# Strassen's seven products for two of the six row tiles in the output matmul of a gated convolution

## The chip, the cores and the metric

The kernel runs on one core of a Trainium2 chip, in float32 throughout. The metric is device time in microseconds, the median of several executions; here 1151.66 us before the change (three runs, 1151.52 to 1152.45). The span of a profile runs from the first to the last instruction, and is a little shorter than the execution's own time.

## What is computed

Two blocks in a row on a batch of 8 sequences of 3136 rows and 256 features: the real part of a two-dimensional Fourier transform, and a feed-forward block with a gate from a three-tap convolution.

```python
X = np.fft.fft(np.fft.fft(x, axis=1), axis=2).real
h = np.maximum(X @ w_in, 0.0)                   # (8, 3136, 1024)
conv_out += conv_w[k] * hp[:, k:k + S, :]       # k = 0, 1, 2; hp is h padded by one row
gate = 1.0 / (1.0 + np.exp(-conv_out))
return h * gate @ w_out                         # (8, 3136, 256)
```

## The kernel before, in words

The transform over the sequence is done by matmuls with cosine and sine tables on a folded input (sums and differences of mirrored rows, so that the tables are an eighth of their size). The transform over the features is folded into w_in: G holds w_in times the feature transform, so that X @ w_in becomes two products, one with the cosine half (tile pt) and one with the sine half (tile qt) of the sequence transform.

The second block is the long part. Each of the 8 batches is cut into 4 **chunks** of rows, each chunk into 8 **steps**, one per 128 of the 1024 hidden features: 256 steps (b, c, f). A step works on 768 or so rows (832 in the last chunk of a batch) in these parts:

- `seed` (ScalarE) writes the first feature's share into a PSUM bank pa, `products` (TensorE) adds the two products in pa and pb, `copies` (ScalarE) moves pb to SBUF as nb, and `combine` (VectorE, two instructions) forms the relu of pa + nb and of pa - nb: the row tile h, both ends of the sequence at once.
- `first_tap` (ScalarE), `middle` (a DMA with addition that GpSimd issues) and `last_tap` (VectorE) make the convolution in tile g; `sigmoid` (ScalarE) and `gate` (VectorE, g times h) finish it.
- `mm2` (TensorE) multiplies the gated step with w_out: g is the stationary operand, 128 rows at a time, and wout of 256 columns the moving one. A chunk has six such **row tiles**; their sums over the 8 steps stay in three PSUM banks po, two tiles in each. After the last step ScalarE copies the banks out and SyncE writes them to DRAM. The last chunk of each second batch has a seventh tile of leftover rows.

A matmul of float32 stands in the profile as two weight loads (PEld) and two passes (PE), so six row tiles are 12 passes of 256 columns.

The program is written as 261 **cycles** (the loop at the end of the function); each engine runs its own instructions strictly in the order written. Cycle t holds, in this order: sigmoid of step t-4, products and copies of step t+1, combine of step t, seed of t+2, first_tap of t, then what is hung on the place "dve" (the folds of the next batch, VectorE instructions of 0.6 to 1.2 us), last_tap of t-3, gate of t-4, what is hung on "late" (the sums that finish a piece of the next batch's sequence transform), middle of t, loads, and mm2 of step t-5, then transform matmuls (tile pd) of the next batch. So the mm2 of cycle t needs the gate that VectorE made in cycle t-1, and VectorE's combine of cycle t needs the products that TensorE made in cycle t-1, ahead of that cycle's mm2. VectorE can thus be about a cycle ahead of what TensorE needs next, and not more. The two PSUM banks pa, the one bank pb and the seven buffers of g set the same limits.

Of the kernel before, what the change touches and what calls it, by code (L numbers as in the profile page):

```python
# [9 lines left out]
F32 = mybir.dt.float32  # L10
# [3 lines left out]
ALU = mybir.AluOpType  # L14
# [23 lines left out]
def kernel(  # L38
# [10 lines left out]
    nc = tc.nc  # L49
    B, S, D = x.shape  # L50
    F = moe_w_in.shape[1]
    P = 128
# [21 lines left out]
    ebp = ctx.enter_context(tc.tile_pool(name="ebp", bufs=4))  # L74
# [6 lines left out]
    edp = ctx.enter_context(tc.tile_pool(name="edp", bufs=1, space=DRAM))  # L81
    psa = ctx.enter_context(tc.tile_pool(name="psa", bufs=2, space=PSUM))
    psb = ctx.enter_context(tc.tile_pool(name="psb", bufs=1, space=PSUM))
    psd = ctx.enter_context(tc.tile_pool(name="psd", bufs=1, space=PSUM))
    pso = ctx.enter_context(tc.tile_pool(name="pso", bufs=4, space=PSUM))

# [5 lines left out]
    def mm(o, l, r, start, stop):  # L92
        nc.tensor.matmul(o, l, r, start=start, stop=stop, skip_group_check=True)  # L93
# [149 lines left out]
    rp = ctx.enter_context(tc.tile_pool(name="rp", bufs=2))  # L243
    PQ, eb, er = {}, {}, {}
    ed = edp.tile([B, (RC // 2 + 1) * RC], F32, name="ed")

# [649 lines left out]
    def keep(s):  # L896
# [3 lines left out]
        if r.start < r.stop:  # L900
            nc.scalar.copy(out=left[:, f, b % 2 * LEFT:(b % 2 + 1) * LEFT], in_=gs[s][:, r])

    def mm2(s):
        b, c, f = s
        ch = chunks[c]
        tiles = [(gs[s][:, o:o + m], [(0, b, r, m)]) for o, r, m in ch.tiles]
        if ch.last and b % 2:
            tiles.append((left[:, f], [(i * LEFT, b - 1 + i, ch.rest[1], LEFT) for i in range(2)]))
        for i, (w, to) in enumerate(tiles):
            if f == 0 and i % 2 == 0:  # L910
                po[b, c, i // 2] = pso.tile([P, 2, D], F32, name="po", tag="po")
            pt = po[b, c, i // 2]
            mm(pt[:, i % 2, :], w, wout[:, f, :], f == 0 and i % 2 == 0, f == NF - 1)
            if f == NF - 1 and (i % 2 or i == len(tiles) - 1):
                del po[b, c, i // 2]
                osb = osp.tile([P, 2, D], F32, name="os", tag="os")
                for j in range(i - i % 2, i + 1):
                    nc.scalar.copy(out=osb[:, j % 2], in_=pt[:, j % 2])  # L918
                if i % 2:
                    r0, r1 = (tiles[j][1][0][2] for j in (i - 1, i))  # L920
                    nc.sync.dma_start(out=bass.AP(
                        tensor=out.tensor, offset=out.offset + (b * S + r0) * D,
                        ap=[[D, P], [(r1 - r0) * D, 2], [1, D]]), in_=osb)
# [3 lines left out]
        gs.pop(s)  # L927


    def keep_on(n):  # L930
# [77 lines left out]
    def at(cycle, where, fn):  # L1008
        side.setdefault((cycle, where), []).append(fn)
# [1 line left out]
    for i in (2, 3):  # L1011
        at((0, 0, 1, 3)[i], "pe", lambda i=i: blocks(i))
    at(0, "pool", store)
    at(0, "load", lambda: spread(0, range(1, len(chunks))))

    early, *rest = three(w_in[2].parts(0, 2, room))
    at(0, "first", early)
# [14 lines left out]
    def free(cycle):  # L1032
# [3 lines left out]
        taken.add(cycle)  # L1036
        return cycle

    feat = Feature()
    at(5, "load", feat.place)  # L1040
    at(8, "dve", feat.signs)
# [10 lines left out]
    for b in range(1, B):  # L1052
        begin, us, *_ = units(b)
        us = us[0:2] + us[5:7] + us[2:4] + us[7:] if b == 1 else us[0:4] + us[5:]

        c0 = ends[b] - 3 * (b == 1)
        n = per * b - (2 if b == 1 else 3) - c0
        at(max(c0, per * (b - 1) + 1), "pe", begin)
        cs = [c0 + i * n // len(us) for i in range(len(us) + 1)]
        if b > 1:  # L1060
            cs[1:] = [c + (-1 if i == len(us) else 1) * (c % NF == LAG % NF) for i, c in enumerate(cs[1:], 1)]
        for i, u in enumerate(us):
            k = cs[i + 1] - cs[i]
# [6 lines left out]
        at(cs[-1] - 2, "load", lambda b=b: spread(b, range(len(chunks) - 1)))  # L1070
        at(per * b + 1, "load", lambda b=b: spread(b, [len(chunks) - 1]))
    for b in range(1, B):
        ops, singles, pres = fold_ops(b)
        c0, n = ends[b - 1], ends[b] - ends[b - 1]
# [130 lines left out]
```

## Time and profile before

| | before |
|---|---|
| median of 3 runs | 1151.66 us |
| profiled execution | 1151.81 us, of it the span 1150.0 us |
| granted TensorE clock | 1.000 |
| busy in the span: PE, PEld | 1133.3 us, 888.3 us |
| busy in the span: VectorE (DVE), ScalarE (ACT), GpSimd (POOL) | 967.9, 894.8, 389.6 us |

The page names each group of instructions by line, engine, operation and tiles (out<-in), with busy time, the mean length of one, and the idle time ahead of it. Lengths overlap: a VectorE instruction may start before the one ahead has ended, and a matmul's end is modelled. What an engine spends on one instruction is therefore read from start to start. The timeline gives these starts. The view by windows gives each engine's busy time between two moments.

### The profile page before, as it was taken

The numbers are of one execution on the slowest core, as the hardware profiler recorded it, in microseconds if no ns is written. First come the engines' busy times: TensorE is split into PE (matmuls) and PEld (weight loads), VectorE is DVE, ScalarE is ACT, GpSimd is POOL, SyncE is SP. The second block draws the span as 40 slices with busy tenths as digits, with TensorE's granted clock in tenths as the row PEclk, the third lists the DMA queues.
The fourth block names the chain that finished last, engine by engine and source line by source line (L and its number), as shares of the span: only waits on it lengthen the run. The fifth ranks groups of instructions, "written<-read, shape, count | busy, mean of one in ns | idle before, by whom it ended". The sixth has DMA issues, their size and how long they took to land.

```text
span 1150.0 us, 15064 instructions
## 1 busy us (share of the span) xinstructions
PE 1133.3 (99%) x4824; PEld 888.3 (77%) x4824; DVE 967.9 (84%) x1452; ACT 894.8 (78%) x1707; POOL 389.6 (34%) x486
## 2 busy tenths in 40 slices
PE   6999999999999999999999999999999999999998
PEld 4777877787778777777778777777778777777777
DVE  8999899988888989898878879888886777777775
ACT  3788778877787778787878777887887777888884
POOL 6425523552434252524143332422222112222223
PEclk9999999999999999999999999999999999999999
DMA  9787975876767677756676766866664656666664
GB/s 249 184 130 158 170 179 110 186 166 143 172 133 151 128 188 157 163 123 150 139 174 134 159 139 129 179 124 123 138 131 87 129 123 142 132 137 124 127 117 100
DMA packets 107676, 167.49 MB, mean 146 GB/s; under 512 B 32175, under 2 KB 62921, under 8 KB 107598
## 3 DMA queue, kind: packets, MB, share of 16 engines
q0 software_dynamic: 42240, 115.87, 52.3%
q1 hardware_dynamic: 64616, 50.53, 15.8%
q8 instruction: 38, 0.62, 0.2%
q10 hardware_dynamic: 741, 0.14, 0.1%
q14 instruction: 41, 0.33, 0.1%
HBM read 37.80 MB, written 25.74 MB: 55 GB/s over the span
## 4 chain that ended last, share of the span: by engine, by line
PE 94%; DVE 3%; ACT 1%; issue 1%; DMA 0%; POOL 0%; DVEq 0%; ACTq 0%
PE po L93 58%; PE pb L93 15%; PE pa L93 15%; PE pd L93 6%; DVE g L863 1%; DVE h L848 1%; DVE g L890 1%; DMA raw<-in_moe_w_in_dram 0%; DVE wout L661 0%; ACT nb L840 0%; DVE raw L667 0%; ACT os L918 0%; ACT g L882 0%; ACT pa L819 0%; ACT g L854 0%
## 5 line engine op out<-in xcount | busy, mean ns | idle before, releaser
L93 PE MATMUL po<-wout,g 128*128 128x256 f32 x3072 | 705.0, 379 | 1.2 <-DVE g L890 1.1
L93 PEld LDWEIGHTS po<-wout,g 128*128 128x128 f32 x3072 | 581.5, 190 | 142.2 <-issue 18.5
L858 POOL DMA_DIRECT2D g<-h x256 | 220.1, 860 | 713.5 <-ACT g L854 474.8
L840 ACT ACTIVATE nb<-pb 128x386 f32<-128x386 f32 (+3 forms) x512 | 228.0, 500 | 196.8 <-PE pb L93 195.8
L848 DVE CUSTOM_DVE_ANT_0 h<-pa,nb 128x386 f32<-128x386 f32 (+3 forms) x512 | 265.4, 560 | 49.3 <-PE pa L93 30.3
L890 DVE TENSOR_TENSOR g<-g,h 128x770 f32<-128x770 f32 (+1 forms) x248 | 240.8, 971 | 64.1 <-ACT g L882 62.3
L863 DVE SCALAR_TENSOR_TENSOR g<-h,cw,g 128x770 f32<-128x770 f32 (+1 forms) x256 | 265.4, 1037 | 1.9 <-DMA g<-h 1.9
L882 ACT ACTIVATE g<-g,cw 128x770 f32<-128x770 f32 (+3 forms) x264 | 246.3, 936 | 18.0 <-DVE g L863 17.9
L854 ACT ACTIVATE g<-h,cw 128x770 f32<-128x770 f32 (+1 forms) x256 | 244.3, 954 | 0.0
L93 PE MATMUL pb<-qt,G 127*128 127x387 f32 (+2 forms) x512 | 213.6, 498 | 1.5 <-ACT nb L840 1.1
L93 PE MATMUL pa<-pt,G 128*128 128x387 f32 (+2 forms) x512 | 212.1, 495 | 0.9 <-ACT pa L819 0.7
L819 ACT ACTIVATE pa<-eb,ge 128x387 f32<-128x387 f32 (+2 forms) x256 | 155.4, 607 | 0.6 <-ACT ft L585 0.3
L93 PEld LDWEIGHTS pa<-pt,G 128*128 128x128 f32 x512 | 96.6, 189 | 75.7 <-issue 19.0
L129 POOL DMA_INDIRECT xh<-in_x_dram,idx x64 | 102.9, 1608 | 19.3 <-issue 10.4
L93 PEld LDWEIGHTS pb<-qt,G 127*128 127x128 f32 x512 | 91.7, 190 | 9.1 <-ACT nb L840 2.8
L93 PE MATMUL pd<-tab,w 98*128 98x197 f32 (+2 forms) x448 | 95.3, 317 | 0.0
L93 PEld LDWEIGHTS pd<-tab,w 98*128 98x128 f32 (+1 forms) x448 | 80.5, 191 | 8.2
L918 ACT COPY os<-po 128x256 f32<-128x256 f32 x196 | 57.5, 394 | 6.3 <-PE po L93 6.3
L176 POOL COPY w<-xh 98x4 f32<-98x4 f32 (+1 forms) x30 | 45.0, 1501 | 6.8 <-DVE xh L170 6.7
L154 DVE TENSOR_TENSOR xh<-xh 98x1020 f32<-98x1020 f32 (+1 forms) x32 | 38.7, 1211 | 0.5 <-DMA xh<-in_x_dram,idx 0.4
L165 DVE TENSOR_TENSOR xh<-xh 98x1024 f32<-98x1024 f32 (+1 forms) x32 | 38.9, 1216 | 0.1
L398 DVE TENSOR_TENSOR as<-as,pd 128x196 f32<-128x196 f32 x14 | 5.0, 358 | 20.4 <-ACT as L394 20.3
(150 smaller groups left out, 427.7 us busy)
## 6 DMA issues: line engine op xcount, KB each, us to landing
g<-h POOLq DMA_DIRECT2D x192, 385.0 KB, 4.0
g<-h POOLq DMA_DIRECT2D x64, 416.0 KB, 4.1
out_dram<-os SPq DMA_DIRECT2D x96, 256.0 KB
xh<-in_x_dram SPq DMA_DIRECT2D x16, 784.0 KB
eb<-ed SPq DMA_DIRECT2D x16, 193.5 KB
raw<-in_moe_w_in_dram SPq DMA_DIRECT2D x4, 512.0 KB
raw<-in_moe_w_out_dram SPq DMA_DIRECT2D x1, 2048.0 KB
eb<-ed SPq DMA_DIRECT2D x8, 209.0 KB
```

The costliest lines, as they stand in the source:

```text
L93: nc.tensor.matmul(o, l, r, start=start, stop=stop, skip_group_check=True)
L129: nc.gpsimd.indirect_dma_start(out=xh[b, h][0:NP, 7 - m].rearrange("p q d -> p (q d)"), out_offset=None, in_=bass.AP(tensor=x.tensor, offs ...
L176: nc.gpsimd.tensor_copy(w[k, 0:2, qs, 0], t()[k, s:s + 2, :, 0])
L819: act(pa[s][:, 0:n], eb[b, c], AF.Copy, scale=ge[:, f:f + 1])
L840: act(nb[s][:, i, cols], p[:, cols], AF.Copy, scale=-1.0 if i else 1.0)
L848: nc.vector._custom_dve(TENSOR_ADD_SAT, out=to, in0=a[:, cols], in1=c[:, i, cols], s0=BIG, s1=0.0)
L854: act(gs[s], hs[s][:, 0:n], AF.Copy, scale=cw[:, 0, s[2]:s[2] + 1])
L858: nc.gpsimd.dma_start(out=gs[s], in_=hs[s][:, 1:1 + n], accum_op=ALU.add)
L863: stt(out=g, in0=h[:, k:k + n], scalar=cw[:, k, f:f + 1], in1=g, op0=ALU.mult, op1=ALU.add)
L882: act(gs[s][:, c], gs[s][:, c], AF.Sigmoid, scale=cw[:, 1, s[2]:s[2] + 1])
L890: vt(g, g, h[:, 0:r.stop], op=ALU.mult)
L918: nc.scalar.copy(out=osb[:, j % 2], in_=pt[:, j % 2])
```

## The change

In 23 of the 32 chunks (all from batch 1's second chunk on, but for the last chunk of batches 1, 3, 5 and 7) the row tiles 4 and 5 are no longer multiplied with w_out step by step. Two steps f-1 and f, f odd, are taken together: the 256 rows of the two tiles by 256 features form a 2 by 2 array of blocks of 128 by 128, a11 to a22, and the two steps' rows of w_out with their two column halves form b11 to b22. Strassen's scheme in Winograd's form gives the product with seven block products in place of eight:

- `forms` (VectorE, once): four combinations of w_out's blocks, in tile tw.
- `sums` (VectorE, in each odd step's cycle, ahead of last_tap): four combinations of the a blocks, 128x128 each, in tile sv, which has one buffer.
- `mm7` (TensorE): three products of 128 columns right after the four other row tiles of the odd step, and four more, which need the sums, at the head of the next step's mm2 (list `due`). All seven are added up over the four pairs of steps in two PSUM banks x and y.
- at the chunk's end ScalarE copies one block, and `end` (VectorE, in the next cycle, behind gate and "late") makes the four output blocks with four instructions that read PSUM; SyncE then writes them.

The banks po per such chunk are four (two for the row tiles 0 to 3, x and y) of the pool's four. Some buffers are given up for room (tile eb from 4 to 3, rt from 2 to 1), and the eb loads are issued a few cycles later.

```diff
+    def sums(s):
+        (a11, a12), (a21, a22) = blocks_of(s)
+        t = sums_of[s] = svp.tile([P, 4, P], F32, name="sv", tag="sv")
+        vt(t[:, 0], a21, a22, op=ALU.add)
+        vt(t[:, 1], a21, a11, op=ALU.subtract)
+        vt(t[:, 2], t[:, 1], a22, op=ALU.add)
+        vt(t[:, 3], a12, t[:, 2], op=ALU.subtract)
...
+    def mm7(s):
...
+        mm(x[:, 0], a11, wout[:, f - 1, 0:P], m == 0, last)
+        mm(x[:, 1], a12, wout[:, f, 0:P], False, last)
+        mm(y[:, 0], a22, TW[4][:, m], m == 0, last)
+        def rest():
+            t = sums_of.pop(s)
+            mm(y[:, 1], t[:, 0], TW[5][:, m], False, last)
+            mm(y[:, 2], t[:, 1], TW[7][:, m], False, last)
+            mm(x[:, 2], t[:, 2], TW[6][:, m], False, last)
+            mm(x[:, 3], t[:, 3], wout[:, f, P:D], False, last)
+        due.append(rest)
...
+        nc.scalar.copy(out=o[:, 1, 0], in_=x[:, 0])
+        def end():
+            twice = lambda w: w.unsqueeze(1).to_broadcast([P, 2, P])
+            vt(o[:, 0], twice(o[:, 1, 0]), x[:, 1:3], op=ALU.add)
+            vt(o[:, 1], twice(o[:, 0, 1]), y[:, 1:3], op=ALU.add)
+            vt(o[:, 0, 1], o[:, 1, 0], x[:, 3], op=ALU.add)
+            vt(o[:, 1], twice(o[:, 1, 1]), y[:, 0:2], op=ALU.add)
+            write(b, c, (4, 5), osb)
+        ends_of.append(end)
     def mm2(s):
...
+        for fn in due:
+            fn()
...
+        if seven(s):
+            tiles = tiles[:4]
...
         run("dve")
+        if t >= LAG and seven(steps[t - LAG]) and steps[t - LAG][2] % 2:
+            sums(steps[t - LAG])
         if 0 <= t - 3 < n:
             last_tap(steps[t - 3])
```

On TensorE, a cycle pair in the first chunk of batch 2 as it stood before (an odd step's mm2, then an even one's; pd is the next batch's transform, x6 means six in a row):

```order
L93 MATMUL po<-wout,g 128x256 [waits DVE_49]
L93 MATMUL po<-wout,g 128x256 x5
L93 MATMUL pd<-tab_109,w 128x197 [waits DVE_49,PE_49,Activation_49]
L93 MATMUL pb<-qt,G 128x387 [waits PE_49]
L93 MATMUL pa<-pt,G 128x387 [waits Activation_49]
L93 MATMUL po<-wout,g 128x256 x6
```

The same place after the change:

```order
L94 MATMUL po<-wout,g 128x256 [waits DVE_49]
L94 MATMUL po<-wout,g 128x256 x3
L94 MATMUL po<-wout,g 128x128 [waits DVE_49,PE_49]
L94 MATMUL po<-wout,g 128x128
L94 MATMUL po<-tw,g 128x128
L94 MATMUL pd<-tab_112,w 128x197 [waits DVE_49,PE_49,Activation_49]
L94 MATMUL pb<-qt,G 128x387 [waits PE_49]
L94 MATMUL pa<-pt,G 128x387 [waits Activation_49]
L94 MATMUL po<-tw,sv 128x128 x3
L94 MATMUL po<-wout,sv 128x128
L94 MATMUL po<-wout,g 128x256 x4
```

Twelve matmuls of 256 columns became eight of 256 and seven of 128; four of the seven stand behind the next step's products.

On VectorE, the same chunk's cycle with a fold (xh) before:

```order
L848 ISA h<-pa,nb 128x386 [waits DVE_49,PE_49,Activation_49]
L848 ISA h<-pa,nb 128x386 [waits Activation_49]
L169 TENSOR_TENSOR xh<-xh 98x512
L170 TENSOR_TENSOR xh<-xh 98x512
L863 TENSOR_SCALAR g<-h,cw,g 128x770 [waits DMASW4_49]
L890 TENSOR_TENSOR g<-g,h 128x770 [waits Activation_49]
```

And after, where DVE_49 is VectorE's own semaphore:

```order
L849 ISA h<-pa,nb 128x386 [waits DVE_49,PE_49,Activation_49]
L849 ISA h<-pa,nb 128x386 [waits Activation_49]
L170 TENSOR_TENSOR xh<-xh 98x512
L171 TENSOR_TENSOR xh<-xh 98x512
L933 TENSOR_TENSOR sv<-g 128x128 [waits DVE_49,PE_49]
L934 TENSOR_TENSOR sv<-g 128x128
L935 TENSOR_TENSOR sv<-sv,g 128x128 [waits DVE_49]
L936 TENSOR_TENSOR sv<-g,sv 128x128 [waits DVE_49]
L864 TENSOR_SCALAR g<-h,cw,g 128x770 [waits DMASW4_49]
L891 TENSOR_TENSOR g<-g,h 128x770 [waits Activation_49]
```

The four sums stand ahead of last_tap and gate, and two of them wait for VectorE's own instruction just ahead. Where a chunk has ended, the next cycle holds behind its gate:

```order
L891 TENSOR_TENSOR g<-g,h 128x770 [waits Activation_49]
L971 TENSOR_TENSOR os<-os,po 128x256 [waits DMAHW3_49,DMAHW4_49,DMAHW0_49,PE_49]
L972 TENSOR_TENSOR os<-os,po 128x256 [waits DVE_49]
L973 TENSOR_TENSOR os<-os,po 128x128 [waits DVE_49]
L974 TENSOR_TENSOR os<-os,po 128x256 [waits DVE_49]
L849 ISA h<-pa,nb 128x386 [waits Activation_49] x2
```

Nothing stood between gate and combine there before.

More of the change, by code (lines that the diff above doesn't have):

```diff
@@ L242 @@
     turn = const.tile([P, 3, 2], F32, name="turn")
[L243 removed]
+    rp = ctx.enter_context(tc.tile_pool(name="rp", bufs=1))
     PQ, eb, er = {}, {}, {}
@@ L901, in keep, with seven, forms @@
             nc.scalar.copy(out=left[:, f, b % 2 * LEFT:(b % 2 + 1) * LEFT], in_=gs[s][:, r])
+    TW = {}
+    due, ends_of = [], []
+    def seven(s):
+        b, c, f = s
+        return (b, c) > (1, 0) and not (chunks[c].last and b % 2)
+    def forms(i):
+        one, two = wout[:, 0:NF:2], wout[:, 1:NF:2]
+        b11, b12, b21, b22 = one[:, :, 0:P], one[:, :, P:D], two[:, :, 0:P], two[:, :, P:D]
+        if i == 0:
+            t = erp.tile([P, 4, NF // 2, P], F32, name="tw", tag="er")
+            TW.update({k: t[:, j] for j, k in enumerate((5, 7, 6, 4))})
+        k, x, y = ((5, b12, b11), (7, b12, b22), (6, b11, TW[7]), (4, b21, TW[6]))[i]
+        vt(TW[k], x, y, op=ALU.subtract)
@@ new lines, in blocks_of @@
+    def blocks_of(s):
+        b, c, f = s
+        o = [chunks[c].tiles[i][0] for i in (4, 5)]
+        return [[gs[b, c, k][:, v:v + P] for k in (f - 1, f)] for v in o]
+    sums_of = {}
+    def sums(s):
[5 more added lines that the diff above has]
+        vt(t[:, 3], a12, t[:, 2], op=ALU.subtract)
@@ L905, in mm2 @@
         ch = chunks[c]
+        done = ends_of[:]
+        for fn in due:
+            fn()
+        due.clear()
+        ends_of.clear()
         tiles = [(gs[s][:, o:o + m], [(0, b, r, m)]) for o, r, m in ch.tiles]
@@ L919, in mm2 @@
                 if i % 2:
[L920 to L923, printed above, removed]
+                    write(b, c, (i - 1, i), osb)
                 else:
@@ L926, in mm2 @@
                         (nc.scalar if j and s == steps[-1] else nc.sync).dma_start(out=rows[b_ * S + r:b_ * S + r + m, :], in_=osb[p0:p0 + m, 0])
-        gs.pop(s)
+        if not seven(s):
+            gs.pop(s)
+        elif f % 2:
+            mm7(s)
+            gs.pop(s)
+            gs.pop((b, c, f - 1))
+        for fn in done:
+            fn()
     def keep_on(n):
@@ L1013 @@
     at(0, "pool", store)
-    at(0, "load", lambda: spread(0, range(1, len(chunks))))
+    at(0, "load", lambda: spread(0, range(1, len(chunks) - 1)))
+    at(NF, "load", lambda: spread(0, [len(chunks) - 1]))
     early, *rest = three(w_in[2].parts(0, 2, room))
@@ L1037, in free @@
         return cycle
+    for i in range(4):
+        at(per + 6 + i, "dve", lambda i=i: forms(i))
     feat = Feature()
```

23 lines of the change are left out of this document (20 added, 3 removed).

## The prediction

> **What bounds the kernel now.** I read the page first: busy times, then the chain that ended last.
>
> ```profile
> span 1150.0 us, 15064 instructions
> PE 1133.3 (99%) x4824; PEld 888.3 (77%) x4824; DVE 967.9 (84%) x1452; ACT 894.8 (78%) x1707; POOL 389.6 (34%) x486
> PE 94%; DVE 3%; ACT 1%; issue 1%; DMA 0%; POOL 0%; DVEq 0%; ACTq 0%
> ```
>
> TensorE carries 94% of the chain, so matmul time saved is time saved, as long as nothing else becomes late. VectorE, which gets the new work, is second with 84%. A share over the whole span hides the stages, so next come windows: seven chunks each (batch 2 to the third chunk of 3; batch 4 to the third of 5; batch 6 to the third of 7), the two chunks of batch 1 that change, the chunk ahead of these, and a stretch of batch 0. Columns: window, length, busy time of PE, PEld, DVE, ACT, POOL.
>
> ```profile
> 340.60:580.40 239.80, 239.80 (x1026) 190.01 (x1025) 210.98 (x317) 189.70 (x352) 87.07 (x97) 1.00 0.70 153
> 617.20:855.00 237.80, 237.80 (x1013) 187.92 (x1012) 203.87 (x307) 189.67 (x351) 66.43 (x87) 1.00 0.66 138
> 891.80:1119.40 227.60, 227.60 (x948) 177.76 (x947) 170.67 (x242) 185.18 (x337) 49.64 (x66) 1.00 0.62 127
> 232.60:268.50 35.90, 35.90 (x158) 28.80 (x157) 31.85 (x50) 27.20 (x52) 17.54 (x16) 1.00 0.69 155
> 268.50:305.70 37.20, 37.20 (x164) 29.82 (x163) 31.29 (x49) 27.28 (x51) 8.79 (x11) 1.00 0.68 147
> 201.20:232.60 31.40, 31.38 (x129) 24.20 (x128) 30.34 (x45) 26.58 (x50) 17.80 (x20) 1.00 0.81 179
> 60.00:90.00 30.00, 28.90 (x115) 21.08 (x114) 29.83 (x47) 25.36 (x54) 9.19 (x17) 1.00 0.83 134
> ```
>
> TensorE never rests in the first five, at full clock (1.00). VectorE's room differs: 28.8 us in the first stretch of seven chunks (4.1 per chunk), 33.9 in the second, 56.9 in the third. The last row shows the other regime: VectorE busy for 29.83 of 30 us, and there TensorE waits.
>
> Who waits for whom in each regime is in the timeline:
>
> ```profile
> 67.63 0.95 DVE L890 TENSOR_TENSOR g<-g,h 128x770 f32<-128x770 f32 x1
> 68.64 2.86 PE L93 MATMUL po<-wout,g 128*128 128x256 f32 x12
> 604.02 1.01 DVE L890 TENSOR_TENSOR g<-g,h 128x832 f32<-128x832 f32 x1
> 604.01 2.75 PE L93 MATMUL po<-wout,g 128*128 128x256 f32 x12
> 606.60 0.59 PE L93 MATMUL po<-wout,left 128*128 128x256 f32 x2
> 608.68 2.75 PE L93 MATMUL po<-wout,g 128*128 128x256 f32 x12
> ```
>
> In batch 0 the gate ends at 68.58 and mm2 starts 0.06 later: TensorE follows VectorE. In batch 3 the gate ends at 605.03 and its mm2 starts at 608.68: VectorE **leads by 3.6 us**. This lead is what it may lose before TensorE feels it.
>
> **TensorE's gain.** 12 passes start within 606.60 - 604.01 = 2.59 us, 0.216 per pass of 256 columns. Per pair of steps, 8 such passes (1.727 us) go and 14 passes of 128 columns come. By columns alone that would be 0.108 each, but each needs its own weight load of 128 columns. What a load costs when the pass is short shows where the passes have 98, 99 and 1 columns, and 196 or 197; of the first two groups I quote the first and the last row of five and of six at even distance:
>
> ```profile
> 30.99 0.30 PEld L93 LDWEIGHTS po<-tab,w 99*128 99x128 f32 x2
> 31.43 0.30 PEld L93 LDWEIGHTS po<-tab,w 98*128 98x128 f32 x2
> 21.34 0.30 PEld L93 LDWEIGHTS po<-dm,win 128*128 128x128 f32 x2
> 21.90 0.19 PEld L93 LDWEIGHTS po<-dm,win 128*128 128x128 f32 x1
> 22.98 4.22 PE L93 MATMUL po<-tab,w 98*128 98x196 f32 x24
> 27.04 2.96 PE L93 MATMUL po<-tab,h 98*128 98x197 f32 x16
> ```
>
> With 99 columns the loads are 0.44 / 4 = 0.110 apart, with one column 0.56 / 5 = 0.112, and with 196 or 197 columns the passes are (27.04 - 22.98) / 24 = 0.169 apart. So there is a floor of 0.111 us per load, whatever the pass, and 128 columns stand just below it. The cost lies between 0.108 (columns alone) and 0.128 (a straight line from 99 to 197 columns). I take the floor, the nearest row: 14 x 0.111 = 1.554, which saves 0.173 per pair; 23 chunks have 92 pairs: **-15.9 us**. By the two ends it is -19.8 and +6.0.
>
> The Trainium skill's page "TensorE: Matmul & The Clock Gate", section "The mechanism", says that a weight load overlaps a running matmul only when the two use different row groups. By that rule each short pass would cost its 0.108 and the 0.111 of its load; 14 of them are 3.07 us, and 92 pairs would add 123 us. The 12 passes in 2.59 us speak against it: load and pass use all rows and still overlap in full.
>
> **VectorE's cost.** How long a 128x128 instruction takes, and what a wait for VectorE's own previous instruction adds:
>
> ```profile
> L157 DVE TENSOR_TENSOR xh<-xh 98x8 f32<-98x8 f32 x8 | 1.4, 171 | 0.0
> L400 DVE TENSOR_TENSOR as<-pd,as 128x196 f32<-128x196 f32 x7 | 2.5, 354 | 0.0
> L428 DVE TENSOR_TENSOR pt<-as 128x392 f32<-128x392 f32 x8 | 4.6, 572 | 0.3
> 623.22 0.35 DVE L424 TENSOR_TENSOR as<-as,pd 128x196 f32<-128x196 f32 x1
> 623.60 0.57 DVE L428 TENSOR_TENSOR qt<-as 128x392 f32<-128x392 f32 x1
> 624.09 0.56 DVE L430 TENSOR_TENSOR qt<-as 128x392 f32<-128x392 f32 x1
> ```
>
> Between 8 elements (171 ns) and 196 (354), 128 take about 285; between 196 and 392, 256 take about 418. L430 needs nothing of L428 and starts 0.08 before that ends (0.49 after a start of 0.57 length); L428 needs L424's result and starts 0.03 after its end. An instruction therefore occupies its length less 0.08 when the next is independent, and its length plus 0.03 when the next waits for it. Of the sums, two of three followers wait: 0.20 + 0.32 + 0.32 + 0.20 = **1.04 us per pair** (0.82 if no wait cost, 1.28 if all did). `end` waits at each of its steps: 0.45 + 0.45 + 0.32 + 0.34 = 1.56 us per chunk. Together 4 x 1.04 + 1.56 = **5.7 us per chunk**, against 4.1 us of room in the first stretch.
>
> The Trainium skill's page "VectorE: DVE Perf Modes", section "The DRAIN you can't avoid", has it that a semaphore between two VectorE instructions costs nothing extra, since the pipe drains anyway. By that the chunk's sum would be 4.4 us. The rows above show 0.11 between the two cases, and the measurement decides.
>
> **What of it lies on the path.** VectorE's busy time counts the last 0.08 of an instruction ahead of a wait, about 50 times in seven chunks, some 4 us, which a VectorE that is never idle doesn't spend.
>
> - First stretch: VectorE needs 211.0 - 4 + 7 x 5.73 = 247.1; TensorE 239.8 - 28 x 0.173 = 235.0. VectorE falls behind by 12.1, the lead takes 3.6: **8.5 us lost**.
> - Second: 203.9 - 4 + 40.1 = 240.0 against 233.0: 7.0 - 3.6 = **3.4 lost**. The chunk between the two (six whole row tiles and a seventh, no sums) lets VectorE win its lead back.
> - Third: 170.7 + 40.1 = 210.8 against 222.8: nothing. Batch 1: `forms`, four instructions of 512 elements (some 2.4 us), and two chunks, 30.3 + 31.9 + 31.3 - 2 + 2.4 + 11.5 = 105.4 against 31.4 + 73.1 - 1.4 = 103.1: 2.3, within the lead.
>
> The rest I cost at nothing. The seven products' waits for sums: the sums stand ahead of the gate that the same mm2 needs for its other tiles. ScalarE loses one copy per chunk; its copy of x must be done before `due` writes there again:
>
> ```profile
> 443.14 1.75 ACT L918 COPY os<-po 128x256 f32<-128x256 f32 x6
> 445.43 1.24 PE L93 MATMUL po<-wout,g 128*128 128x256 f32 x5
> ```
>
> Five copies end near 444.7, and `due` reaches x after 445.4: 0.7 us or more of cover, at most 23 times that if it goes. The eb loads come 14 cycles ahead of their use. The output DMA waits for `end`, and what SyncE has behind it (loads of x and eb) is needed cycles later.
>
> Sum against the profiled execution: 1151.8 - 15.9 + 8.5 + 3.4 = **1147.8 us**; that execution stands 0.15 above the median of the runs.
>
> **The rivals.**
>
> 1. *VectorE stays hidden*, because its waits for itself cost nothing (7 x 4.44 = 31.1 us in the first stretch: 238.1 against 235.0, within the lead) or the lead is longer. 1151.8 - 15.9 = 1135.9. For it: 16% of VectorE's time is idle. Against: the 0.11 us above, and the windows. 0.17.
> 2. *VectorE becomes the clock, with no lead to spend* (slower): the sums stand ahead of last_tap and gate, so the odd steps' gates, which mm2 waits for, come late by themselves, and sigmoid, which needs last_tap, with them. Then all excess counts: 12.1 + 7.0 + 2.3 = 21.4, and 1151.8 - 15.9 + 21.4 = 1157.3. It decides where VectorE needs more per chunk than TensorE's 33.6, that is from 28 us of old work on, which both stretches exceed. For it: 60 to 90 us. Against: the lead of 3.6. 0.24.
> 3. *The short passes cost the straight line's 0.128*: TensorE +6.0, the first stretch's excess falls to 247.1 - 241.6 - 3.6 = 1.9, the second's to nothing: 1159.7. Against: the floor is the same at 1 and at 99 columns. 0.10.
> 4. *Loads and passes in series*, by the page's rule: about 1275. 0.01.
>
> That the change does nothing is excluded by the order of instructions, which holds all 644 short matmuls.
>
> **How the numbers follow.** The forecast has 0.48, with 1141 to 1153 as its own range (VectorE's added work 10% cheaper or dearer, 3 to 4 us in each stretch). 0.2%, about what a measurement of this kernel can tell from no change, is 2.3 us: 1149.4 to 1154.0. Of the forecast's chance 0.30 lies below and 0.18 within; rival 1 is below; of rival 2, 0.03 within and 0.21 above; of rival 3, 0.03 and 0.07; rival 4 above. Faster 0.47, same 0.24, slower 0.29. The range 1136 to 1160 leaves out some of rival 1's half below it, the dearer half of 2, and 4.
>
> **What would show it.** 14 short passes 0.111 us apart; sums at 1.04 us and `end` at 1.56; VectorE busy without a break in batches 2, 3 and 5, with mm2 starting within 0.1 us of a gate's end there, and TensorE without waits in batches 6 and 7, where seven chunks shorten by 4.8 us. I am wrong in the gain if the short passes stand 0.12 or more apart, and in the loss if VectorE has idle time in batch 3, or if batches 6 and 7 don't shorten.

## The result and the profile after

The change makes the kernel **slower**: 1164.8 us (median of 4 runs, 1163.61 to 1166.44) against 1151.73 before (4 runs), a ratio of 1.0113 with the interval 1.0096 to 1.0131. The forecast was 1147.8, and the range ended at 1160. The rival that comes nearest by its number is the third with 1159.7, but its dearer short passes are not there (0.111 us each, below). The second, in which VectorE becomes the clock, gave 1157.3; it has the right engine, and the time is 7.5 us above that too. One execution of e11 below ran at a mean granted clock of 0.754 (1476 us) and is left out of its median.

The page of the profile after (this execution took 1166.44 us), with the last line from the chain that ended last:

```profile
span 1164.7 us, 16738 instructions
PE 1127.2 (97%) x5376; PEld 895.6 (77%) x5376; DVE 1080.1 (93%) x1916; ACT 889.9 (76%) x1684; POOL 375.1 (32%) x486
PE 18%; ACT 0%; issue 0%
```

VectorE went from 84% to 93%. TensorE is busy for 6 us less and still has a longer span. The chain, followed back from the end, is TensorE's unbroken run for 18% of the span and breaks off there.

The windows that answer to those of before, each from the start of the same steps' first mm2 (seven chunks of batches 2 and 3, of 4 and 5, of 6 and 7; then the first chunk of batch 1, the two after it that change, and the plain one; a **plain chunk** is one without the seven products). The columns are those of the prediction's table:

```profile
346.40:592.30 245.90, 237.83 (x1191) 191.27 (x1190) 242.40 (x453) 189.73 (x346) 78.38 (x97) 1.00 0.69 150
630.50:872.60 242.10, 235.69 (x1177) 190.29 (x1176) 236.28 (x444) 189.05 (x345) 60.90 (x87) 0.99 0.65 136
909.80:1134.20 224.40, 223.21 (x1112) 178.69 (x1111) 201.66 (x379) 183.53 (x332) 50.34 (x67) 1.00 0.64 131
201.60:236.80 35.20, 33.13 (x130) 25.25 (x129) 34.32 (x50) 26.99 (x50) 21.11 (x20) 0.95 0.73 166
236.80:310.40 73.60, 72.08 (x367) 58.80 (x367) 69.90 (x133) 55.28 (x101) 21.20 (x27) 1.00 0.69 152
310.40:346.40 36.00, 35.21 (x149) 27.40 (x148) 32.85 (x49) 27.56 (x57) 19.01 (x23) 1.00 0.65 138
```

In the first stretch VectorE is busy for 242.40 of 245.90 us. What is left is 0.8 us at the stretch's very start and, behind that, 78 gaps of some 0.03 us ahead of instructions that wait for VectorE's own result. The second stretch has 0.5 us at its start and three longer gaps, 2.6 us together. TensorE stands still for 8.1 and 6.4 us where it never rested before. Only the third stretch is shorter than before, by 2.9 us (from the start of one first mm2 to the next; the windows are set by up to 0.8 us ahead of these) and not by the 4.8 of its short products. The fourth row holds a surprise: a chunk without any of the seven products is 3.8 us longer.

For whom TensorE waits is in its view of waits (us in total, times, longest; two waits at the kernel's start are left out):

```profile
PE pd L94 <- DVE qt L383: 5.9, 5, 1.5
PE pd L94 <- DVE as L371: 4.4, 3, 1.7
PE pd L94 <- DVE as L425: 3.1, 2, 2.5
PE pa L94 <- ACT pa L820: 2.8, 3, 2.1
PE pd L94 <- DVE as L428: 2.5, 3, 1.1
PE po L94 <- DVE g L891: 1.6, 2, 1.1
PE po L94 <- DVE os L973: 1.3, 2, 0.9
```

The gate (L891), at which the prediction looked for the loss, has 1.6 us. Of the 56 steps of the first stretch two start their mm2 within 0.1 us of the gate's end, and of the 56 of the second none, where the prediction expected this as the sign of the loss. The waits stand at **pd**, the transform matmuls of the next batch: this bank has one buffer, and it comes free when VectorE has read the last piece out of it with the finishing sums on "late". One such place, in the first steps behind batch 4's last chunk, in the timeline (start, length, engine, line):

```profile
768.69 0.41 DVE L971 TENSOR_TENSOR os<-os,po 128x256 f32<-128x256 f32 x1
769.14 0.42 DVE L972 TENSOR_TENSOR os<-os,po 128x256 f32<-128x256 f32 x1
769.59 0.29 DVE L973 TENSOR_TENSOR os<-os,po 128x128 f32<-128x128 f32 x1
769.91 0.42 DVE L974 TENSOR_TENSOR os<-os,po 128x256 f32<-128x256 f32 x1
770.25 1.02 DVE L849 CUSTOM_DVE_ANT_0 h<-pa,nb 128x385 f32<-128x385 f32 x2
771.19 0.28 DVE L933 TENSOR_TENSOR sv<-g 128x128 f32<-128x128 f32 x1
771.38 0.28 DVE L934 TENSOR_TENSOR sv<-g 128x128 f32<-128x128 f32 x1
771.71 0.29 DVE L935 TENSOR_TENSOR sv<-sv,g 128x128 f32<-128x128 f32 x1
771.96 0.39 PE L94 MATMUL po<-tw,g 128*128 128x128 f32 x2
772.03 0.29 DVE L936 TENSOR_TENSOR sv<-g,sv 128x128 f32<-128x128 f32 x1
772.24 1.01 DVE L864 SCALAR_TENSOR_TENSOR g<-h,cw,g 128x770 f32<-128x770 f32 x1
773.17 0.95 DVE L891 TENSOR_TENSOR g<-g,h 128x770 f32<-128x770 f32 x1
774.04 0.35 DVE L424 TENSOR_TENSOR as<-as,pd 128x196 f32<-128x196 f32 x1
774.31 0.35 DVE L425 TENSOR_TENSOR as<-as,pd 128x196 f32<-128x196 f32 x1
774.81 0.44 PE L94 MATMUL pd<-tab,w 99*128 99x99 f32 x2 [2.46 <-DVE as L425]
```

VectorE runs without a gap from `end` (L971 to L974) through combine, the four sums and last_tap to the gate; the two instructions that read pd stand behind all of them. TensorE is done with its last short pass at about 772.3 and gets pd at 774.81. It needs VectorE there **in the same cycle** in which that gate is made, while the mm2 that uses this gate comes a cycle later.

TensorE's short passes themselves, in batch 7:

```profile
1026.29 0.83 PE L94 MATMUL po<-tw,sv 128*128 128x128 f32 x6
1026.96 0.39 PE L94 MATMUL po<-wout,sv 128*128 128x128 f32 x2
1027.18 1.89 PE L94 MATMUL po<-wout,g 128*128 128x256 f32 x8
```

Six passes in 0.67 us and two in 0.22: 0.111 each, as forecast. The gain is there; it is given back elsewhere.

To follow it through the experiments I use one number for each kernel, worked out from the trace's records: TensorE's **stops**, the time by which two passes start further apart than the first one's columns (or the floor of 0.111 us) take, added up from 100 us on wherever it is over 0.03 us. A pass at half the clock counts with its excess. Before: 2.0 us. After: 31.2, of which 20.7 at pd in 34 places. The short products' -15.9 and 29.2 more stops make +13.3 us; measured were +13.1. The stops say where the time went, not why; that is for the experiments.

### The profile page after: what moved, and what is told of

Same layout as the page of the kernel before. It is cut to its first block, busy times and chain, and to the rows that moved or that the text cites. A ratio compares the mean times of both kernels' runs of the same rounds, so it can differ in the third digit from the quotient of the medians.

```text
span 1164.7 us, 16738 instructions
## 1 busy us (share of the span) xinstructions
PE 1127.2 (97%) x5376; PEld 895.6 (77%) x5376; DVE 1080.1 (93%) x1916; ACT 889.9 (76%) x1684; POOL 375.1 (32%) x486
## 5 line engine op out<-in xcount | busy, mean ns | idle before, releaser
L94 PE MATMUL po<-wout,g 128*128 128x256 f32 (+1 forms) x2704 | 590.0, 366 | 2.9 <-DVE g L891 1.6
L94 PEld LDWEIGHTS po<-wout,g 128*128 128x128 f32 x2704 | 491.8, 190 | 104.9 <-issue 12.6
L891 DVE TENSOR_TENSOR g<-g,h 128x770 f32<-128x770 f32 (+1 forms) x248 | 240.6, 970 | 22.5 <-ACT g L883 22.5
L130 POOL DMA_INDIRECT xh<-in_x_dram,idx x64 | 99.1, 1548 | 19.3 <-issue 13.8
L94 PEld LDWEIGHTS po<-tw,sv 128*128 128x128 f32 x552 | 76.3, 192 | 27.0 <-issue 8.5
L94 PEld LDWEIGHTS pd<-tab,w 98*128 98x128 f32 (+1 forms) x448 | 74.8, 190 | 24.5 <-issue 10.2
L94 PE MATMUL po<-tw,sv 128*128 128x128 f32 x552 | 76.9, 276 | 0.0
L1000 ACT COPY os<-po 128x256 f32<-128x256 f32 x150 | 44.4, 393 | 7.6 <-PE po L94 7.6
```

Of the source, the lines that this page charges most:

```text
L130: nc.gpsimd.indirect_dma_start(out=xh[b, h][0:NP, 7 - m].rearrange("p q d -> p (q d)"), out_offset=None, in_=bass.AP(tensor=x.tensor, offs ...
L891: vt(g, g, h[:, 0:r.stop], op=ALU.mult)
```

## The experiments

The theories. **A**: the early release of pd is a wait of its own; move it, and most of the loss goes. **C** (called **D** in the later runs, where it comes with numbers): VectorE's whole work is the clock in the stretches where it is saturated; pd is only the place where its lateness shows first. **B**: the short products cost TensorE more than forecast whatever VectorE does. The kernel before was measured beside each group of runs; its medians were 1151.55 (e1, e2, e4, e5), 1152.55 (e3, e6, e7, e8) and 1151.84 us (e9 to e11).

### e1: no sums

```diff
-        t = sums_of[s] = svp.tile([P, 4, P], F32, name="sv", tag="sv")
-        vt(t[:, 0], a21, a22, op=ALU.add)
...
+        if not fixed:
+            fixed.append(svp.tile([P, 4, P], F32, name="sv", tag="sv"))
+            nc.gpsimd.memset(fixed[0], 0.5)
+        sums_of[s] = fixed[0]
```

It leaves out the four sums of each pair: four of the seven products multiply a constant tile.

> The changed kernel without the sums: tile sv is filled once with a constant and the four late products of each pair read it, so TensorE's instructions are the same 644 short matmuls and VectorE is spared 92 x 1.04 = 96 us; `end` stays. It leaves out four of the seven products' operands. Theory A (VectorE's added work makes its finishing sums of the transform late, and TensorE waits for the one bank pd that they hold): pd waits fall from 20.7 us to under 3, and the time is 1151.7 - 15.9 for TensorE, plus some 4 for the chunk with a seventh row tile that waits for `end`'s banks: 1140. Rival B (the short products themselves, their banks or their loads cost more than their 0.111 us): 1155 or more.

Measured: **1140.84 us** (1139.49 to 1142.18), ratio 0.9903 (0.9886 to 0.9919). Stops fall to 6.7 us, at pd to 0.5. The seven products, `end` and `forms` together are worth -10.7 us; the sums on VectorE, with the waits for them, cost 24 us. The three stretches are 4.3, 4.6 and 4.6 us shorter than before, which is the forecast gain of 4.8 nearly whole. B falls.

### e2: the transform's matmuls one cycle later

```diff
-            k = cs[i + 1] - cs[i]
+            late = 1 if b > 1 and i and cs[i + 1] - cs[i] > 1 else 0
+            k = cs[i + 1] - cs[i] - late
...
-                at(cs[i] + j, "pe", lambda u=u, j=j, k=k: u.matmuls(j, k))
+                at(cs[i] + late + j, "pe", lambda u=u, j=j, k=k: u.matmuls(j, k))
```

> The changed kernel, with one edit: from batch 2 on, each piece of the next batch's transform starts its matmuls one cycle later than the sums that finish the piece before, so that the bank pd is free by then. All of VectorE's work stays. Theory A (the wait for pd costs the time, because it needs VectorE a whole cycle earlier than mm2's gates do): nearly all of the 20.7 us of pd waits go, and what remains lost is what VectorE's total exceeds TensorE's by, some 12 us by the sum of the forecast, so 1150 to 1155. Rival C (VectorE's total work is the clock, and pd is only where the wait shows): the waits move to the gates, and the time stays at 1161 or above.

Measured: **1162.08 us** (1161.54 to 1163.44), ratio 1.0094 (1.0077 to 1.011). Its waits, a piece of its timeline and the clock right behind that:

```profile
PE po L94 <- DVE g L891: 9.5, 12, 1.4
PE po L94 <- DVE os L973: 3.8, 3, 2.3
```

```profile
593.90 1.53 PE L94 MATMUL po<-wout,g 128*128 128x256 f32 x4 [2.30 <-DVE os L973]
```

```profile
594.00:598.00 4.00, 4.00 (x11) 2.98 (x12) 3.13 (x5) 0.00 (x0) 0.00 (x0) 0.57 0.70 166
```

The stops at pd fall from 20.7 to 2.1 us, and those at po (gates and `end`'s banks) rise from 7.0 to 19.8. **A falls** as the main cause: its range was 1150 to 1155, and the time fell by 2.6 us alone (+13.1 became +10.5; the intervals of the two ratios overlap, so this size is rough). By stretches the profiled execution shows where pd matters by itself: the third, in which VectorE has room, is 4.6 us shorter than before and no longer 2.9. This kernel also shows what VectorE's lead is worth when it is really spent. The second stretch takes 237.8 us where it took 242.1 in the kernel after, so 4.3 are won (the first wins 1.4). But the plain chunk ahead of it takes 41.3 (38.3 in after, 37.1 before) and the one behind it 38.5 (37.1): its first step needs a bank that the late `end` still holds, TensorE stands for 2.30 us at 593.90, and the granted clock is 0.57 in the four microseconds that follow, another 4 x (1 - 0.57) = 1.7 us. What a stretch borrows from the lead, the next plain chunk pays back.

### e3: the same edit in the kernel before

> The kernel before with the transform's matmuls one cycle later from batch 2 on: a control for the same edit in the changed kernel. VectorE is ahead there and no pd wait is seen: no difference, 1150 to 1153. If the edit itself costs something (longer bursts of transform matmuls in one cycle), it shows here.

The edit is that of e2, in the kernel before. Measured: **1152.54 us**, ratio 1.0000 (0.9991 to 1.001). By itself the later start costs and brings nothing, so e2's 2.6 us belong to the change.

### e4: the sums on GpSimd

```diff
-        vt(t[:, 0], a21, a22, op=ALU.add)
+        gt(t[:, 0], a21, a22, op=ALU.add)
```

and so for all four.

> The changed kernel with its four sums per pair on GpSimd in place of VectorE. GpSimd's own multiply of 128x448 takes 1.26 us in the profile, so that four of 128x128 take perhaps 2 to 3 us per pair; GpSimd is busy for a third of the time. Theory A: VectorE then has only `end` more than before, and the time is near 1140, as without sums. Against it stands that the sums may delay the DMA issues of the middle tap behind them on GpSimd, and last_tap with them: then 1150 to 1165, with VectorE waiting for the DMA.

Measured: **1163.02 us** (1160.97 to 1164.67), ratio 1.0093 (1.0076 to 1.011). Groups of instructions (count, busy us, mean ns) and a wait of this kernel:

```profile
L934 POOL TENSOR_TENSOR sv<-g 128x128 f32<-128x128 f32 x92 | 119.7, 1301 | 0.0
L933 POOL TENSOR_TENSOR sv<-g 128x128 f32<-128x128 f32 x92 | 98.9, 1075 | 0.7
L935 POOL TENSOR_TENSOR sv<-sv,g 128x128 f32<-128x128 f32 x92 | 67.6, 735 | 7.2
L936 POOL TENSOR_TENSOR sv<-g,sv 128x128 f32<-128x128 f32 x92 | 67.5, 734 | 7.2
```

```profile
PE po L94 <- POOL sv L936: 6.4, 5, 1.9
```

A pair's sums take 1.08 + 1.30 + 0.74 + 0.73 = 3.85 us there, against 1.05 on VectorE, and I had expected 2 to 3. TensorE now stops 13 us for the sums themselves, and VectorE waits 24.2 us for GpSimd's writes at the ends of h (L826), which stand behind the sums there (10.1 us before). The time lies in the second of the expected ranges, 1150 to 1165, but not by a DMA that comes late. Freeing VectorE helped, and the slower engine took it back; this run alone tells neither A from C nor either from a limit of GpSimd.

### e5 and e6: seven products only in batches 6 and 7; then `forms` late as well

e5, and e6 with the second edit added:

```diff
-        return (b, c) > (1, 0) and not (chunks[c].last and b % 2)
+        return b >= 6 and not (chunks[c].last and b % 2)
```

```diff
-        at(per + 6 + i, "dve", lambda i=i: forms(i))
+        at(6 * per + i, "dve", lambda i=i: forms(i))
```

> The seven products only in batches 6 and 7 (7 chunks of the 23), where VectorE has 57 us of room in seven chunks. Theory A: each of the seven chunks gains 4 x 0.173 us, the pd waits of batch 6 (1.6 us) and the wait of the last chunk for `end`'s banks (1.1) take some back: 1151.7 - 4.8 + 2.7, 1148 to 1150. Rival B (short products cost more than they save): 1152 or more.

> The seven products only in batches 6 and 7, as in the run before, with one more edit: `forms` (four VectorE instructions of 512 elements) moves from batch 1's first chunk to batch 6's first cycles, where VectorE has room. In the run before, batch 1's first chunk took 3.8 us longer than in the kernel before although nothing but `forms` was new there: TensorE waited 2.1 us for a seed, and the granted clock then stood at half for 3.4 us. Theory: that goes, 1152.1 - 3.8 = 1148.3. Rival (the loss in that chunk comes from the eb loads or buffers that were also changed): no difference, 1152.

Measured: e5 **1152.10 us** (1150.83 to 1153.57), ratio 1.0002 (0.9993 to 1.0012); e6 **1149.74 us** (1149.48 to 1150.88), ratio 0.9977 (0.9968 to 0.9986). e5 missed its 1148 to 1150 and lies where B would have it (1152 or more); e6 shows that it isn't the short products. The four instructions of `forms`, 2.4 us of VectorE's time, cost 0.25% or 2.9 us of the whole by the ratios (3.4 by the medians) where the change puts them, in the first chunk of batch 1. e6 came out 1.4 us above its 1148.3; the kernel before was 1.0 us slower beside it than beside e5. How `forms` cost this is seen in the kernel after:

```profile
218.61 3.02 POOL L177 COPY w<-xh 99x4 f32<-99x4 f32 x1
221.71 0.91 ACT L222 ACTIVATE rt<-w,turn 98x256 f32<-98x256 f32 x2 [3.62 <-POOL w L179]
223.14 1.58 PE L94 MATMUL pa<-pt,G 128*128 128x387 f32 x2 [2.07 <-ACT pa L820]
```

```profile
222.00:226.00 4.00, 2.86 (x6) 1.97 (x7) 3.52 (x7) 4.00 (x9) 2.38 (x3) 0.66 0.26 66
226.00:230.00 4.00, 4.00 (x17) 3.04 (x16) 3.95 (x7) 2.67 (x6) 1.59 (x2) 0.92 0.94 189
```

With `forms` ahead of them, GpSimd's copy of w starts 2.7 us later than before (215.91 there; 0.5 of it because the chunk itself starts later). ScalarE stands for 3.62 us at an instruction that needs it (1.56 before), the seed queued behind that is late, the products that add to its bank pa wait 2.07 us, and then the clock is down: 4 x (1 - 0.66) + 4 x (1 - 0.92) = 1.7 us more. No gate was late there (the smallest lead is 0.55 us). In e2 and e9 the same wait of 2.07 us stands at the same place, the clock stays at 1.00 behind it, and the chunk is 2.1 us longer than before in place of 3.7: the wait costs 2.1 us each time, the half clock 1.7 in some executions only. e6 without this wait is the first version that beats the kernel before.

### e7: the first two sums exchanged

The third sum waits for the second; when the first stands between them, one wait of VectorE for itself is gone.

```diff
-        vt(t[:, 0], a21, a22, op=ALU.add)
         vt(t[:, 1], a21, a11, op=ALU.subtract)
+        vt(t[:, 0], a21, a22, op=ALU.add)
         vt(t[:, 2], t[:, 1], a22, op=ALU.add)
```

> The changed kernel with the first two of the four sums exchanged, so that the one that waits for the difference a21 - a11 no longer stands right behind it: one of the two waits for VectorE's own last instruction goes, 0.11 us per pair, 10 us over 92 pairs, 3.1 in each stretch of seven chunks. Theory D (VectorE's total work is the clock in the stretches from batch 1 to 5, whatever TensorE's wait is put down to): the time falls by what these chunks hold, 64 x 0.11 = 7 us at most, 1158 to 1160. Theory A (only the bank pd, which the finishing sums free, makes TensorE wait): these sums come earlier by 0.11 only where they share a cycle with the four sums, so less than 3 us, 1162 to 1165.

Measured: **1157.35 us** (1156.68 to 1158.31), ratio 1.0040 (1.0024 to 1.0055). The same place behind batch 4 as in the timeline above, where the sums and last_tap started 0.19, 0.33, 0.32 and 0.21 apart (1.05 in all):

```profile
765.71 0.28 DVE L933 TENSOR_TENSOR sv<-g 128x128 f32<-128x128 f32 x1
765.91 0.28 DVE L934 TENSOR_TENSOR sv<-g 128x128 f32<-128x128 f32 x1
766.11 0.28 DVE L935 TENSOR_TENSOR sv<-sv,g 128x128 f32<-128x128 f32 x1
766.42 0.29 DVE L936 TENSOR_TENSOR sv<-g,sv 128x128 f32<-128x128 f32 x1
766.63 1.01 DVE L864 SCALAR_TENSOR_TENSOR g<-h,cw,g 128x770 f32<-128x770 f32 x1
```

Here they start 0.20, 0.20, 0.31 and 0.21 apart, 0.92 in all. 0.13 us less per pair, with two instructions exchanged and none taken out, gave 8.3 us against the kernel before measured beside it (+13.1 became +4.8). That is more than D's range (1158 to 1160) and far more than A's. In the 64 pairs of the stretches where VectorE is saturated and of batch 1 it would be 0.13 for 0.13. The profiled executions show it by stretches: 3.1 us in the first and 4.1 in the second, 28 pairs each (the half clock at 776 in the kernel after, 1.7 us, has no like in e7's second stretch), and 0.3 in the third, where VectorE has room. **C and D are borne out**: where VectorE is saturated, a tenth of a microsecond of its work is about a tenth of the total.

### e8: every other chunk

```diff
-        return (b, c) > (1, 0) and not (chunks[c].last and b % 2)
+        return (b >= 6 or b >= 2 and c % 2 == 1) and not (chunks[c].last and b % 2)
...
-        at(per + 6 + i, "dve", lambda i=i: forms(i))
+        at(per + 24 + i, "dve", lambda i=i: forms(i))
```

> The seven products in every second chunk of batches 2 to 5 (six chunks, each with an unchanged one ahead of it) and in batches 6 and 7 (seven chunks), `forms` in batch 1's last chunk. Theory D: a chunk of 5.7 us more on VectorE is followed by one with 4 us of room, and VectorE keeps up: 13 x 0.69 = 9.0 us gained, perhaps 4 lost to waits for pd and for `end`'s banks: 1145 to 1149. Theory A alone: pd is waited for in each such chunk for 1 to 2.5 us as in the changed kernel: 1150 to 1155.

Measured: **1150.85 us** (1150.55 to 1150.97), ratio 0.9985 (0.9976 to 0.9994): faster than before, but 2 us above what D gave, and inside the 1150 to 1155 of A alone. The waits that A named are not there, though: VectorE has 15 us of gaps in the first stretch again, and TensorE stops 9.0 us in all, 2.9 of it at pd and 4.5 at po. So total work doesn't explain all of it; e11 shows where the rest stands.

### e9, e10, e11: the two edits together

The exchanged sums (e7) and the later transform (e2), put into the kernel after (e9), into e6 (e10) and into e8 (e11).

> All of the change, with the two edits tried apart before put together: the first two sums exchanged (one wait less, 0.11 us per pair of steps) and the transform's matmuls of batches 2 and on one cycle later. Theory D, in which VectorE's whole work is the clock and the place of the wait matters little: the two gains add at most, 1164.8 - 7.4 - 2.7 = 1154.7, and with the sums' order the transform's wait has partly gone already, so 1154 to 1157. Theory A, in which the bank of the transform is a wait of its own: its waits in the exchanged kernel are 14.9 us, which would go nearly whole, to 1142 to 1147.

> Seven products in batches 6 and 7 alone, the forms late, the sums in the cheaper order and the transform's matmuls one cycle later. TensorE's only added waits of the kernel with the forms late were 1.5 us for the transform's bank, at 933.1 and 967.0; both edits take them. D: 1149.7 - 1.5 = 1148.2 (1147.5 to 1148.8), which is the sum of seven chunks at 0.69 less what was there before. Rival: the waits go to other places as they did with all chunks, 1149.4 to 1150.2.

> Seven products in batches 6 and 7 and in every other chunk of 2 to 5 (13 chunks, whose short products save 9.0 us), forms late, with the cheaper order and the transform one cycle later. TensorE waited 9.0 us in this kernel without the two edits: 2.9 us for the transform's bank, and 4.5 us at gates and at the first step of a plain chunk, which needs a bank that the sums of the closing step (`end`) still hold. D (VectorE's work in each stretch decides, and it has room in every other chunk): the transform's 2.3 us go and half of the others, 1146 to 1148.5. Rival (the wait of the plain chunk for the bank that `end` holds is a cost of the change by itself, which no order of the sums takes): 1148.5 to 1150.5.

Measured: e9 **1154.71 us** (1152.65 to 1156.83), ratio 1.0027 (1.0017 to 1.0037); e10 **1147.73 us** (1146.6 to 1148.13), ratio 0.9961 (0.9948 to 0.9973); e11 **1146.44 us** (median of five runs, 1146.14 to 1147.09), ratio 0.9954 (0.9941 to 0.9967).

e9 lies in D's range, near the sum of its two gains (13.1 - 8.3 - 2.6 = 2.2, measured 2.9); A's 1142 to 1147 is excluded once more. e10 has 2.3 us of stops, as good as before, and its gain is that of seven chunks at 0.69 us. In e11 pd's stops are gone and 4.1 us are left at po, 3.2 of them in four stops of plain chunks behind chunks with seven products. The longest, in its timeline, and the first stretch of this kernel in the time of the stretch before:

```profile
480.75 1.10 PE L94 MATMUL po<-wout,g 128*128 128x256 f32 x4 [1.35 <-DVE os L973]
```

```profile
340.60:580.40 239.80, 237.62 (x1095) 190.08 (x1094) 223.18 (x377) 188.02 (x345) 81.59 (x97) 1.00 0.70 151
```

VectorE has room (223.18 of 239.80), and the plain chunk's first step still waits for a bank until L973 has read it. That part is a cost of the change by itself, as the rival said; the time came out as D's. e10 and e11 beat both kernels, by 0.4 and 0.5% of the time before. Where e11 wins is in its stretches: the third is 4.6 us shorter than before, the second 1.4 shorter, the first 0.9 longer. So the six chunks of batches 2 to 5 bring 0.5 us together, and the seven of batches 6 and 7 the rest.

## Why the prediction was wrong

Stops and chunks account for every kernel with the change to within 1.7 us. Chunks x 0.69 us are the gain of the short products; added to it is what the stops have over the 2.0 us of before. The stops are those of the profiled execution, the measured times medians of all; in the profiled executions themselves, from batch 1 on, the two agree to within 0.8 us.

| kernel | chunks | stops, us | gain + added stops | measured (medians) |
|---|---|---|---|---|
| after | 23 | 31.2 | +13.3 | +13.1 |
| e1 no sums | 23 | 6.7 | -11.2 | -10.7 |
| e2 transform later | 23 | 26.7 | +8.8 | +10.5 |
| e4 sums on GpSimd | 23 | 29.0 | +11.1 | +11.5 |
| e5 batches 6, 7 | 7 | 7.5 | +0.7 | +0.6 |
| e6 and forms late | 7 | 3.5 | -3.3 | -2.8 |
| e7 sums' order | 23 | 22.9 | +5.0 | +4.8 |
| e8 every other chunk | 13 | 9.0 | -2.0 | -1.7 |
| e9 after, both edits | 23 | 19.4 | +1.5 | +2.9 |
| e10 e6, both edits | 7 | 2.3 | -4.5 | -4.1 |
| e11 e8, both edits | 13 | 5.1 | -5.9 | -5.4 |

By the prediction's own parts, from the start of one first mm2 to the next (the sums are those of the profiled executions, -4.0 forecast and +14.6 measured):

| part | forecast | measured |
|---|---|---|
| batch 1, three chunks | -1.4 | +4.2 |
| its plain chunk | 0 | +1.1 |
| first stretch of seven | +3.7 | +6.0 |
| plain chunk of batch 3 | 0 | +1.2 |
| second stretch of seven | -1.4 | +4.6 |
| plain chunk of batch 5 | 0 | +0.1 |
| third stretch of seven | -4.8 | -2.9 |
| ahead and behind | 0 | +0.4 |

Of the 18.6 us between the two sums, 8.3 lie in the first two stretches, where the lead had been subtracted; 5.6 in batch 1, most of it from `forms`; 2.4 in the plain chunks; 1.9 in the third stretch; 0.4 elsewhere.

**TensorE's gain: right.** 0.111 per short pass, 0.69 us per chunk (four pairs at 0.173), and e1 shows it in the time. The short passes of the added products stand 0.111 us apart with all rows in use. So the rule of the Trainium skill, "TensorE: Matmul & The Clock Gate", section "The mechanism", that a load overlaps a running matmul only when the row groups differ, stays contradicted.

**VectorE's added work: right.** The sums take 1.05 us (forecast 1.04), and `end` from start to next start 0.45 + 0.45 + 0.32 + 0.34 = 1.56, as forecast. VectorE's need in the two full stretches was put at 247.1 and 240.0; after the change it spent 245.9 - 0.8 = 245.1 and 242.1 - 3.1 = 239.0. The waits for itself count in full (e7). By the Trainium skill, "VectorE: DVE Perf Modes", section "The DRAIN you can't avoid", e7 should have changed nothing, and it changed 8.3 us.

**"The lead takes 3.6 us": the step that failed.** It was subtracted in both stretches and, as "within the lead", in batch 1. The second stretch, forecast to lose 3.4 us, lost 9.1; the first lost 10.9 in place of 8.5. Three things were wrong with the step.

- Its size was read at one gate. Another one of before, in batch 2, in the timeline:

```profile
376.43 0.96 DVE L890 TENSOR_TENSOR g<-g,h 128x770 f32<-128x770 f32 x1 [1.10 <-ACT g L882]
379.80 2.53 PE L93 MATMUL po<-wout,g 128*128 128x256 f32 x11
```

  The gate ends at 377.39 and its mm2 starts at 379.80: 2.4 us. Over all steps of the two stretches before the change the lead is 1.9 us at the least, with a median of 3.6 and 3.8: the gate that was read is a typical one, and the smallest lead is what runs out first.
- It was read at the wrong place. What TensorE asks first of VectorE is the release of pd, in the same cycle as the gate; there were 20.7 us of stops there while the gates had 2.4 and 2.7 us left in the median of the two stretches. Moving pd's need by a cycle (e2) brought 2.6 us in all: where VectorE is saturated, most of the stops moved on to the gates and to `end`'s banks.
- It isn't a gain but a loan. I wrote that the plain chunk lets VectorE win its lead back. The plain chunk is just where the loan is called in: its first step needs `end`'s banks. In e2 the second stretch won 4.3 us, and the two plain chunks around it lost 3.0 and 1.3 against the kernel after.

Without the credit, rival 2's sum holds nearly: the second stretch has 240.0 - 233.0 = 7.0 of excess by the sum (6.0 by the 239.0 of the trace), and 3.1 us on top in which VectorE itself waited; measured were 242.1 - 233.0 = 9.1. Three of these waits, 1.24, 0.68 and 0.68 us, are for ScalarE's copies of transform pieces, in steps where VectorE had waited 1.45, 1.66 and 1.65 us before the change too: the forecast had VectorE without a break there. The first stretch has 12.1 by the sum and 245.9 - 235.0 = 10.9 by the trace. Whether the 1.2 between are lead that was of use once, or a need put a little too high, the traces don't tell.

**`forms`: mis-sized.** They were counted as 2.4 us of VectorE's work in a chunk with room at the gates. The chain that mattered leaves VectorE at another place: through GpSimd's copy and ScalarE's queue to the seed. e6 puts them at 2.9 us, the trace at 3.8, of which 1.7 are half clock.

**The third stretch: 1.9 us missed** though VectorE has 20 us of gaps. It is pd's release again (stops of 0.97 and 0.56 us at 950 and 984, in the cycles behind `end`, where its four instructions, the sums and the gate stand ahead of what reads pd). With pd's need a cycle later, in e2 and e10, this stretch is 4.6 us shorter than before, as forecast within 0.2. A stretch's total says nothing of one cycle.

**Plain chunks: costed at nothing.** "The output DMA waits for `end`, and what is behind it is needed cycles later" looked at DMA queues; the pool's four banks are the shorter supply. A chunk with seven products uses all four, and the next one's first step needs x's at once.

Rival 2 had the right engine and the right condition, but its price left out these banks, `forms` and the clock: 21.4 us of excess in its sum against 29.2 us of stops. Its chance, 0.24, was too low: the argument against it was the lead alone.

Of e2's 4.2 us in the plain chunk 2.30 are the stop for the bank and 1.7 the half clock behind it. Open is whether a fifth bank for po would take this stop away: no run has one.

## What to carry to other kernels

When work goes to the second busiest engine, compare its need with the shorter time of the first engine stage by stage, and count all excess: in this case a lead was spent once, its smallest value counted, and the next stage that shared a buffer took it back. Ask for each thing that the leading engine waits for (banks as well as data) in which cycle it is needed, and put the added work behind the earliest of them or thin it out: here the seven products in batches 6 and 7 and every other chunk ahead of them, with the sums in the order that waits least, turned +13.1 us into -5.4, nearly all of it won where VectorE had room from the start. Waits of a saturated engine for its own previous result count like work, and e7 took one of two away by exchanging two independent instructions.

## What the runs showed of the hardware

- **Half clock after short stops, but not after each.** In the kernel after, behind stops of 2.07 us (223.14) and 2.46 us (774.81) of TensorE, passes stood twice as far apart for 3.4 us (776.1 to 779.6: 0.427 us per pass of 256 columns in place of 0.216), some 1.7 us lost each time; behind the first the windows show it as 0.66 and 0.92. In e2 the same stop of 2.07 us, at 223.19, left the clock whole:

```profile
222.00:226.00 4.00, 2.81 (x12) 2.30 (x13) 3.52 (x7) 4.00 (x9) 2.38 (x3) 1.00 0.23 63
```

  In e9 it did so too (222.76), while a stop of 1.92 us there (589.42) brought half clock (0.62 from 590 to 594). In e4 a stop of 1.95 us (436.58) brought it and one of 1.92 (465.70) did not. In e8, whose longest stop is 1.40 us, the mean granted clock of the whole span is 1.000. So stops of 1.9 to 2.1 us can cost 1.7 us more or nothing more; what decides is not shown by these runs. The Trainium skill, "TensorE: Matmul & The Clock Gate", section "Why this matters for your kernels", warns of gaps over about 3 us; in this case shorter ones were enough at times.
- **A wait of VectorE for its own previous instruction** costs 0.11 to 0.14 us at 128 elements (0.19 to 0.20 against 0.31 to 0.33 from start to start).
- **GpSimd needs 0.73 to 1.30 us** for an addition or subtraction of 128x128 (e4) that takes VectorE 0.28 to 0.29, beside a VectorE that is busy for 89% of the span.
